# Sharing the first normalisation with GpSimd and asking for the weights after it, with the first v on SyncE's queue

## The chip, the cores and the metric

The kernel runs on one core of a Trainium2 chip. The metric is device time in microseconds (us), the median of several executions. The span that a trace shows is some 2 us shorter than that time.

In the views of the profile, PE is TensorE's matmuls, PEld its weight loads, DVE is VectorE, ACT is ScalarE, POOL is GpSimd and SP is SyncE. An "L" with a number is a line of that kernel's own source. A "q" behind an engine is that engine's sequencer.

## The reference

A linear attention over 8 batches, 8 heads, 576 positions and 64 columns a head, followed by two matrix products with a periodic function between them.

```python
def _attn_ref(q, k, v):                       # (8, 8, 576, 64) f32
    q_s = np.exp(q - max);  q_s /= sum over the last axis
    k_s = np.exp(k - max);  k_s /= sum over the positions
    kv = np.einsum('bhsd,bhse->bhde', k_s, v)
    return np.einsum('bhsd,bhde->bhse', q_s, kv)

def _moe_ref(x, w_in, w_out, alpha):          # x (4608, 512), w_in (512, 2048), w_out (2048, 512)
    h = x @ w_in
    s = np.sin(alpha * h)
    g = h + s * s / (alpha + 1e-09)
    return (g @ w_out).astype(np.float32)
```

(The two lines of the softmaxes are shortened.) Each of the two weights is 4.2 MB in f32, and q, k and v are 1.18 MB for each batch.

## The kernel before

The kernel works batch by batch. ACT takes exponentials of q and k, DVE sums and normalises q, PE transposes it and multiplies k by v, and the result goes into `xT`. The two products with the weights then keep PE busy until the end, while the next batches' attention is worked in between. The helpers that matter here are these:

```python
def load_win(c0, c1):                    # two requests for columns c0..c1 of w_in, f32 -> bf16 on the way
    n = slice(c0, c1)
    for x in range(2):
        nc.gpsimd.dma_start(out=win[64 * x:64 * x + 64, :, n], in_=win_v[x][:, :, n])

def load_wout(c):
    nc.gpsimd.dma_start(out=wout[:, 4 * c:4 * c + 4, :], in_=wout_v[:, 4 * c:4 * c + 4, :])

def norm_q(b, engs):                     # for each half ii of the batch's q
    ...
            nc.vector.tensor_reduce(part, qe[:, ii], axis=AXL.X, op=ALU.add)
            nc.vector.reciprocal(part, part)
        engs[ii % len(engs)].tensor_tensor(qn[:, ii]..., qe[:, ii], part..., op=ALU.mult)
```

The prologue asks for q and k on SyncE's queue. GpSimd asks for v and the weights. A copy of one element, called `held`, makes GpSimd wait until the first half of q has landed.

```python
load("q", q, 0, halves=True)             # SyncE
load("k", k, 0, halves=True)             # SyncE
...
GP_CP(singles.tile([128, 1], F32, name="held"), staged["q", 0][:, 0, 0, 0:1])
staged["v", 0] = st = stage.tile([128, 4, J, D], F32, name="st_v", tag="st")
for ii, j0, j1 in ((0, 0, 9), (1, 0, 5), (1, 5, 9)):
    GP.dma_start(out=st[:, ii::2, j0:j1]..., in_=src_view(v, 0)[:, ii::2, j0 * D:j1 * D])
for c0, c1 in ((0, 256), (256, 512), (512, 1024), (1024, 1536), (1536, 2048)):
    load_win(c0, c1)
for c in range(2):
    load_wout(c)
exp_q(0)
exp_k(0)
...
warm_up(7)
norm_q(0, [V, V])                        # both halves on DVE
```

Later loads are tied to the work of the first 512 tokens (`ni` counts its 16 column blocks of w_in). A gate is a tiny write by DVE into the buffer, so that the request waits until DVE has got there.

```python
late = {6: lambda: load("q", q, 1, halves=True, gate=DVE_CP), 8: lambda: load_wout(2),
        10: lambda: load_wout(3), 13: lambda: load("k", k, 1, halves=True, gate=DVE_CP)}
...
load("v", v, 1, halves=True)             # second batch's v, on SyncE behind the gated k
```

The softmax here doesn't subtract the row's maximum and nothing guards it: scores larger than these inputs give would overflow.

## Time and profile before

| | before |
|---|---|
| median of the first 3 runs | 289.12 us (289.1 to 289.53) |
| span of the trace | 286.8 us, of which PE is busy 274.9 |
| first matmuls on the weights | 15.74 us |
| second batch's v landed | 42.77 us |

PE idles for 286.8 - 274.9 = 11.9 us, mostly before 15.74. The one view to add is the timeline of GpSimd in the prologue. Its columns are the start in us, the duration, engine, source line, operation, what it wrote and read, the number of instructions, and in brackets the idle time before it with what ended it.

```profile
5.09 2.32 POOL L295 DMA_DIRECT2D st_v<-in_v_dram  x3
7.40 3.13 POOL L107 DMA_DIRECT2D win<-in_moe_w_in_dram  x5
11.43 0.61 POOL L107 DMA_DIRECT2D win<-in_moe_w_in_dram  x1 [0.90 <-DMA st_v<-in_v_dram]
12.25 2.61 POOL L107 DMA_DIRECT2D win<-in_moe_w_in_dram  x4 [0.21 <-issue]
```

GpSimd wrote requests for weights from 7.40 to 10.53.

### The profile page before, as it was taken

What the parts mean: (1) busy time and instruction counts of PE and PEld (TensorE: products, weight loads), DVE (VectorE), ACT (ScalarE), POOL (GpSimd) and SP (SyncE); (2) the same over time, 40 slices, a digit from 0 to 9 for tenths busy, and PEclk for the clock granted to TensorE, in tenths of its full rate; (3) what the DMA queues carried; (4) which work ended last, traced back from release to release, by engine and by line L of the source; (5) the groups of instructions that cost most, each with busy time, mean ns of one, the idle gap of its engine ahead of it and who ended that gap; (6) DMA issues with size and microseconds to landing.
All of it is one profiled execution on the core that took longest, in us unless ns stands there. A gap on an engine that the chain in (4) does not pass through costs nothing.

```text
span 286.8 us, 4259 instructions
## 1 busy us (share of the span) xinstructions
PE 274.9 (96%) x1570; PEld 130.6 (46%) x1570; DVE 188.5 (66%) x281; ACT 226.6 (79%) x320; POOL 81.6 (28%) x77
## 2 busy tenths in 40 slices
PE   1899999999999999999999999999999999999994
PEld 0444454445454445444544454445444444444443
DVE  3867775899968668756775677757674555555412
ACT  4889756999489999899889988998877777777500
POOL 4859420674766571005300530032000000000000
PEclk9999999999999999999999999999999999999999
DMA  7999999946799957129910990116011111111142
GB/s 253 309 205 242 269 391 408 307 169 191 167 199 402 361 184 120 38 43 358 289 37 21 336 308 27 37 39 139 17 39 37 37 37 39 37 37 38 41 109 73
DMA packets 37381, 45.77 MB, mean 160 GB/s; under 512 B 15968, under 2 KB 20848, under 8 KB 37360
## 3 DMA queue, kind: packets, MB, share of 16 engines
q1 hardware_dynamic: 32032, 39.98, 46.3%
q0 software_dynamic: 5136, 5.38, 10.2%
q8 instruction: 12, 0.20, 0.3%
q10 hardware_dynamic: 192, 0.14, 0.2%
q14 instruction: 9, 0.07, 0.1%
HBM read 36.71 MB, written 9.44 MB: 161 GB/s over the span
## 4 chain that ended last, share of the span: by engine, by line
PE 84%; DMA 7%; DVE 5%; POOL 1%; ACT 1%; issue 1%; SPq 0%; POOLq 0%
PE hp L234 38%; PE op L254 35%; DMA st_v<-in_v_dram 4%; PE hh L234 3%; PE kvp L157 2%; PE xp L206 2%; DMA qT<-qn 2%; DMA st_q<-in_q_dram 1%; DVE qs L144 1%; PE op L532 1%; PE op L234 1%; ACT s L240 1%; DVE qn L146 1%; POOL qn L146 1%; POOL s L244 1%
## 5 line engine op out<-in xcount | busy, mean ns | idle before, releaser
L250 DVE SCALAR_TENSOR_TENSOR g<-s,inva_sb,hp 128x512 bf16<-128x512 f32 x130 | 96.1, 745 | 64.1 <-ACT s L242 54.2
L234 PE MATMUL hp<-xT,win 128*128 128x512 bf16 x520 | 129.7, 379 | 0.0
L254 PE MATMUL op<-wout,g 128*128 128x512 bf16 x496 | 124.2, 379 | 0.0
L240 ACT ACTIVATE s<-hp,alpha_sb 128x512 f32<-128x512 f32 x130 | 87.6, 682 | 25.4 <-PE hp L234 24.3
L234 PEld LDWEIGHTS <-win 128*128 128x128 bf16 x576 | 56.3, 98 | 67.4 <-issue 0.4
L254 PEld LDWEIGHTS <-g 128*128 128x128 bf16 x560 | 54.1, 98 | 61.7 <-issue 0.9
L242 ACT ACTIVATE s<-s 128x512 f32<-128x512 f32 x112 | 70.5, 630 | 3.5
L146 POOL TENSOR_TENSOR qn<-qe,qs 128x1152 bf16<-128x1152 bf16 x12 | 25.3, 2128 | 73.2 <-DVE qs L140 63.1
L244 POOL TENSOR_TENSOR s<-s 128x512 f32<-128x512 f32 x29 | 30.5, 1061 | 24.8 <-ACT s L240 24.3
L260 DVE COPY o<-op 128x512 f32<-128x512 f32 (+2 forms) x33 | 22.1, 669 | 9.6 <-PE op L254 7.1
L117 ACT ACTIVATE ke<-st_k 128x1152 bf16<-128x1152 f32 x16 | 17.9, 1151 | 4.8 <-DMA st_k<-in_k_dram 4.1
L117 ACT ACTIVATE qe<-st_q 128x1152 bf16<-128x1152 f32 x16 | 17.9, 1156 | 2.8 <-DMA st_q<-in_q_dram 2.8
L139 DVE TENSOR_REDUCE qs<-qe 128x36 f32<-128x2304 bf16 x5 | 12.8, 2553 | 8.7 <-ACT qe L117 8.6
L131 POOL CAST vb<-st_v 128x1152 bf16<-128x1152 f32 x12 | 13.6, 1162 | 10.4 <-DMA st_v<-in_v_dram 10.4
L254 PE MATMUL hp<-wout,g 128*128 128x512 bf16 x64 | 15.1, 379 | 0.0
L209 DVE CAST xT<-xp 128x512 bf16<-128x512 f32 (+1 forms) x18 | 13.4, 742 | 0.0
L117 ACT ACT_TABLE_LOAD x7 | 9.0, 1283 | 1.3 <-PEq L546 1.2
L157 PEld LDWEIGHTS <-ke 64*128 64x128 bf16 x288 | 8.2, 93 | 3.5 <-ACT s L242 1.3
L157 PE MATMUL kvp<-vb,ke 64*128 64x130 bf16 x288 | 9.7, 216 | 0.0
L234 PE MATMUL hh<-xT,win 128*128 128x512 bf16 x40 | 9.4, 379 | 0.0
L144 DVE TENSOR_REDUCE qs<-qe 128x18 f32<-128x1152 bf16 x6 | 8.0, 1329 | 2.1 <-ACT qe L117 2.1
L206 PE MATMUL xp<-qT,kbd 128*128 128x256 bf16 (+1 forms) x40 | 8.2, 286 | 0.4 <-DVE xT L209 0.3
(68 smaller groups left out, 117.9 us busy)
## 6 DMA issues: line engine op xcount, KB each, us to landing
out_dram<-o SPq DMA_DIRECT2D x70, 128.0 KB, 2.3
st_q<-in_q_dram SPq DMA_DIRECT2D x6, 1152.0 KB, 6.3
st_k<-in_k_dram SPq DMA_DIRECT2D x6, 1152.0 KB, 8.2
st_v<-in_v_dram SPq DMA_DIRECT2D x6, 1152.0 KB, 10.3
st_q<-in_q_dram SPq DMA_DIRECT2D x4, 576.0 KB, 5.5
st_k<-in_k_dram SPq DMA_DIRECT2D x4, 576.0 KB, 7.1
wout<-in_moe_w_out_dram POOLq DMA_DIRECT2D x4, 512.0 KB, 11.2
win<-in_moe_w_in_dram POOLq DMA_DIRECT2D x6, 256.0 KB, 7.1
```

The costliest lines, as they stand in the source:

```text
L117: nc.scalar.activation(dst[:, :, ii * 128:(ii + 1) * 128].rearrange("p j (x d) -> p x j d", x=2), src[:, ii::2], AX.Exp)
L131: engs[ii](vv[:, 2 * ii:2 * ii + 2, :, 0:D], staged["v", b][:, ii::2])
L146: engs[ii % len(engs)].tensor_tensor(qn[:, ii].rearrange("p j (x d) -> p j x d", x=2), qe[:, ii], part.unsqueeze(3).to_broadcast([128, J, ...
L157: nc.tensor.matmul(kvp[:, e, ii * 130:(ii + 1) * 130], ke[r, j, ii * 128:(ii + 1) * 128], vt[r, j, ii * 130:(ii + 1) * 130], start=(j == 0 ...
L206: nc.tensor.matmul(xp[:, e, 0:n], kt[:, e, ii], qT[:, ii, j0:j1, e * 64:(e + 1) * 64], start=True, stop=True)
L234: nc.tensor.matmul(hp, win[:, ki, ni * 128:(ni + 1) * 128], xT[:, ki, t * MF:(t + 1) * MF], start=(ki == 0), stop=(ki == 3))
L240: nc.scalar.activation(s, hp, AX.Sin, scale=alpha_sb[:, ni:ni + 1])
L242: nc.scalar.activation(s, s, AX.Square)
L244: nc.gpsimd.tensor_tensor(s, s, s, op=ALU.mult)
L250: nc.vector.scalar_tensor_tensor(G[t][:, ni], in0=s, scalar=inva_sb[:, ni:ni + 1], in1=hp, op0=ALU.mult, op1=ALU.add)
L254: nc.tensor.matmul(acc, G[t][:, ni, j * 128:(j + 1) * 128], wout[:, ni, :], start=(ni == 0), stop=(ni == nN - 1))
L260: eng(o[:, cols], acc)
```

## The change

The intent is to finish the first batch's q earlier by giving one half of its normalisation to GpSimd, which only issued requests until then. The weights' requests follow that product on GpSimd. The first v would have had to wait too, so SyncE asks for it, behind k. One copy moves from ACT to DVE, and PE's warm-up matmuls are distributed anew.

```diff
     load("k", k, 0, halves=True)
+    staged["v", 0] = st = stage.tile([128, 4, J, D], F32, name="st_v", tag="st")
+    for ii, j0, j1 in ((0, 0, 9), (1, 0, 5), (1, 5, 9)):
+        nc.sync.dma_start(out=st[:, ii::2, j0:j1].rearrange("p i j d -> p i (j d)"),
+                          in_=src_view(v, 0)[:, ii::2, j0 * D:j1 * D])
 ...
-    GP_CP(singles.tile([128, 1], F32, name="held"), staged["q", 0][:, 0, 0, 0:1])
-    (v's three requests on GpSimd, the same as above)
+    exp_q(0)                             # these and two helpers only change place
+    exp_k(0)
+    ...
+    warm_up(9)
+    norm_q(0, [GP, V])
+    q_tile(0)
     for c0, c1 in ((0, 256), (256, 512), (512, 1024), (1024, 1536), (1536, 2048)):
         load_win(c0, c1)
     for c in range(2):
         load_wout(c)
 ...
-    warm_up(7)
-    norm_q(0, [V, V])
-    q_tile(0)
     q_transpose_ii(0, 0, 0, 8, tps[0])
 ...
-    warm_up(6)
+    warm_up(1)
 ...
-    ACT_CP(A["qT", 0][:, 1, 0:8], tps[1])
+    DVE_CP(A["qT", 0][:, 1, 0:8], tps[1])
```

(The lines in brackets and the comments stand for what is left out.)

More of the change, by code (lines that the diff above doesn't have):

```diff
@@ L289 @@
     nc.vector.reciprocal(inva_sb, alpha_sb)
-    GP_CP(singles.tile([128, 1], F32, name="held"), staged["q", 0][:, 0, 0, 0:1])
-    staged["v", 0] = st = stage.tile([128, 4, J, D], F32, name="st_v", tag="st")
-    for ii, j0, j1 in ((0, 0, 9), (1, 0, 5), (1, 5, 9)):
-        GP.dma_start(out=st[:, ii::2, j0:j1].rearrange("p i j d -> p i (j d)"),
-                     in_=src_view(v, 0)[:, ii::2, j0 * D:j1 * D])
-    for c0, c1 in ((0, 256), (256, 512), (512, 1024), (1024, 1536), (1536, 2048)):
-        load_win(c0, c1)
-    for c in range(2):
-        load_wout(c)
     exp_q(0)
@@ L312, in cast_v0 @@
         eng(vv[:, 2 * ii:2 * ii + 2, j0:j1, 0:D], staged["v", 0][:, ii::2, j0:j1])
-    warm_up(7)
-    norm_q(0, [V, V])
+    warm_up(9)
+    norm_q(0, [GP, V])
     q_tile(0)
+    for c0, c1 in ((0, 256), (256, 512), (512, 1024), (1024, 1536), (1536, 2048)):
+        load_win(c0, c1)
+    for c in range(2):
+        load_wout(c)
     q_transpose_ii(0, 0, 0, 8, tps[0])
```

## The prediction

> **What bounds the kernel now.** I read the page first: the engines' shares, then the chain that ended last.
>
> ```profile
> PE 274.9 (96%) x1570; PEld 130.6 (46%) x1570; DVE 188.5 (66%) x281; ACT 226.6 (79%) x320; POOL 81.6 (28%) x77
> PE 84%; DMA 7%; DVE 5%; POOL 1%; ACT 1%; issue 1%; SPq 0%; POOLq 0%
> ```
>
> TensorE is busy 274.9 of 286.8 us and makes 84% of the chain. Nothing in the change removes a useful matmul, so only the 11.9 us in which PE is idle can shrink, and the change touches the first batch alone: the first 16 us. Second I read the order of time there. These are DVE's lines for the first batch's q (columns: start us, us, engine, line, operation), then for the second batch, where DVE and GpSimd already share the normalisation just as the change wants it for the first; the POOL line belongs to that second batch.
>
> ```profile
> 6.13 1.35 DVE L144 TENSOR_REDUCE qs<-qe 128x18 f32<-128x1152 bf16 x1 [2.13 <-ACT qe L117]
> 7.82 1.36 DVE L146 TENSOR_TENSOR qn<-qe,qs 128x1152 bf16<-128x1152 bf16 x1
> 10.78 1.36 DVE L146 TENSOR_TENSOR qn<-qe,qs 128x1152 bf16<-128x1152 bf16 x1
> ...
> 34.74 1.34 DVE L144 TENSOR_REDUCE qs<-qe 128x18 f32<-128x1152 bf16 x1
> 37.93 1.97 DVE L146 TENSOR_TENSOR qn<-qe,qs 128x1152 bf16<-128x1152 bf16 x1
> ...
> 36.56 2.13 POOL L146 TENSOR_TENSOR qn<-qe,qs 128x1152 bf16<-128x1152 bf16 x1 [4.56 <-DVE qs L145]
> ```
>
> DVE alone needs 6.13 to 12.14 for both halves; shared, 34.74 to 39.90. Third, what follows on PE and ACT:
>
> ```profile
> 12.20 0.73 PE L186 MATMUL tp<-identb,qn 128*128 128x128 bf16 x10 [1.04 <-DVE qn L146]
> 12.86 1.20 PE L157 MATMUL kvp<-vb,ke 64*128 64x130 bf16 x36
> 15.74 1.95 PE L234 MATMUL hp<-xT,win 128*128 128x512 bf16 x8
> ...
> 10.31 0.99 ACT L319 COPY qT<-tp 128x1024 bf16<-128x1024 bf16 x1
> 11.20 0.74 ACT L312 CAST vb<-st_v 128x640 bf16<-128x640 f32 x1
> ```
>
> From 15.74 on PE runs without a gap to the second batch. So the start of those first `hp` matmuls is what the prologue delivers. Fourth, the chain in order of time around the second batch (start, us, what):
>
> ```profile
> 32.24 10.53 DMA st_v<-in_v_dram
> 42.77 0.02 issue
> 42.79 0.76 DVE vb L131
> 43.55 0.59 DVE o L260
> ...
> 44.92 0.55 PE xp L214 x2
> ```
>
> The second batch's v is requested at 32.24 and lands only at 42.77, and PE's attention matmuls at 44.92 hang on it. Why 10.5 us for 0.59 MB? The table by stretches (last columns: DMA share, GB/s):
>
> ```profile
> 3.00:8.00 5.00, 2.10 (x6) 0.97 (x7) 2.22 (x5) 2.46 (x3) 3.03 (x5) 1.00 1.04 403
> 9.00:11.00 2.00, 1.93 (x15) 0.95 (x14) 1.93 (x4) 1.78 (x3) 1.53 (x3) 1.00 0.96 368
> 11.00:13.00 2.00, 0.96 (x17) 0.70 (x18) 1.88 (x3) 1.33 (x3) 1.37 (x2) 1.00 1.14 221
> 14.00:24.00 10.00, 9.37 (x45) 4.04 (x44) 7.16 (x14) 9.17 (x17) 6.17 (x8) 1.00 1.26 205
> 38.00:42.80 4.80, 4.80 (x42) 2.64 (x41) 3.34 (x4) 3.76 (x4) 0.69 (x1) 1.00 1.04 410
> ```
>
> The DMA engines are full from 3 us to beyond 42.8 us. The weights count here as the bf16 written; they are read as f32, so 205 GB/s is 410 read. What must pass before that v has landed: three batches' halves q, k, v twice, 6 x 1.18 = 7.1 MB, and both weights, 8.4 MB as f32: 15.5 MB, at 0.405 MB/us some 38 us, from 3 to 41. That is the landing at 42.77 but for about a microsecond of notice. So there are **two bounds in series**: the prologue's chain of engines to 15.74, and the DMA stream to 42.77.
>
> **What the Trainium skill says.** "SBUF — State Buffer", section "Who interferes with whom": a VectorE instruction with two SBUF inputs contends with a GpSimd instruction that reads SBUF, and the second of them to start waits for the whole of the first. The trace agrees: GpSimd ran to 36.56 + 2.13 = 38.69, and DVE's multiplication, 1.36 us alone, took 1.97 and ended at 39.90, 1.21 after GpSimd. "GPSIMD Engine Reference", section "3.1 Elementwise — side-by-side cycle accounting": a two-input tensor_tensor in f32 is 1.96 times slower on GpSimd; here, with a broadcast factor, it is 2.13 / 1.36 = 1.57 times. "DMA: Bandwidth & Descriptors", section "SWDGE vs HWDGE vs iDMA": requests of SyncE and GpSimd end on the same 16 engines; GpSimd writes descriptors in software and VectorE's two-port modes can lock it out meanwhile. The stretches agree on the first (403 and 410 on the hardware queue, 2 x 205 on the other); on the second there is a hint: the one weight request beside DVE's two casts at 12.06 took 0.78 us, the shortest took 0.62. The same page, "Specifications", has the first byte of a GpSimd request after about 1 us, of a SyncE one after 0.6; this trace can't tell, since the engines were full when GpSimd first asked.
>
> **The change part by part.**
> 1. GpSimd takes the first half. The first reciprocal ends at 7.52 + 0.27 = 7.79. In the second batch GpSimd began 0.17 after it, so 7.96, and 2.13 gives 10.09, where DVE gave 9.18: this half is **0.9 later**.
> 2. DVE keeps the second half and follows the second batch's pattern: 39.90 - 34.74 = 5.16 after 6.13, so 11.29 instead of 12.14: **0.85 earlier**.
> 3. PE transposes the first half at 10.15 to 10.77. ACT's copy, 10.31 before, begins at about 10.82 and the v cast behind it at 11.71 (copy to cast takes 0.89 as before), done at 12.45 instead of 11.94. The second half's ten transposes run 11.35 to 12.08. The k-v matmuls wait for ACT's cast: 12.50 instead of 12.86. So **0.36 earlier**, not 0.85.
> 4. The copy of the second transposed half (ACT, 1.00 us) goes to DVE. DVE has the two v casts (0.82 us for both) from 11.29 to 12.11 and this copy, about 0.7 by the 0.75 of a 1152-column one, to 12.85. It is free when the k-v result comes (13.59 - 0.36 = 13.23). No cost, and ACT is free for its v cast at 12.35 to 12.98.
> 5. v on SyncE's queue: four q and k halves landed 1.46 us apart (4.92 to 9.2), so v lands at 10.7, 11.5 and 12.1 against 11.1, 12.0 and 12.6 before. In the kernel before ACT idled 0.67 for the last piece, which the k-v matmuls used only later; now it lands ahead of ACT.
> 6. The weights are requested from 10.1 instead of 7.4. They could not move before v was through at about 11.7 in the kernel before. Now v is through at 8.5 + 1.18/0.405 = 11.4, and the first weights follow at an estimated 11.5 to 12 (10.09 plus one issue of 0.62, or the skill's 1 us, plus some). Needed is the first piece at 15.1 and the 512 to 1024 columns at 18.7, two issues and 2.1 MB after: at 0.41 MB/us, 17 to 17.6 plus 0.9 notice. Close, but in time.
> 7. Matmuls of warm-up: 7 + 6 become 9 + 1, in PE's idle time; they set no end.
>
> So `hp` starts at about 15.4. **But** that gain of 0.36 meets the second bound. The landing at 42.77 moves only if the stream moves. The kernel before lost, against 405, about 0.2 us in 9 to 11 us and 0.4 in 11 to 13: 0.6 us. The changed one wins this back with v on the hardware queue and pays an estimated 0.1 to 0.6 of gap after v, and up to 0.4 while DVE's casts disturb the second to third request, with no backlog to hide it. Sum: **0 +- 0.5 us** at 42.77. PE, 0.36 early, then waits there, and the end stays: 289.1.
>
> **Rivals.** (a) *The prologue's gain carries through*: 289.12 - 0.36 = 288.75, if v lands 0.4 earlier. For it: the lost 0.6 us. Against: GpSimd asks 2.7 us later. (b) *The weights come late*: GpSimd's first request after 10.1 needs 2.5 us, as requests under load do (the first of 5.09 moved nothing before 8.4, when k was through), v drains at 11.4, the engines idle for 1.2 us: the second batch's v lands 0.6 to 1 later, perhaps with a wait for `win` near 18.7: 289.8 to 290. For it: latencies of 2.4 to 3.4 us everywhere in this trace; against: all of those were behind a backlog. (c) *GpSimd becomes the bound*: its requests now end near 10.1 + 10 x 0.63 + 0.37 + 1.51 = 18.3, and its first square came at 19.06, 18.7 when PE is early. No wait expected; 0.3 us if the lock costs more.
>
> **Range and chances.** All terms are under 1 us, 2% is 5.8 us. Point 289.1, range 288.5 (rival a with a bit more) to 289.9 (rival b). Faster by over 2%: 0.01; within: 0.98; slower: 0.01.
>
> **What would show it.** Right: GpSimd's product 7.96 to 10.1, DVE's ending near 11.3 and lasting 1.97, `hp` starting near 15.4 and no PE wait on `win`; the second batch's v landing at 42.3 to 43.3, and PE's gap before the attention matmuls near 45 grown from 0.1 to some 0.5 us. Wrong: DMA share under 0.8 in 11 to 13 us (rival b), an earlier landing with the end earlier by as much (a), a first square after 19 behind GpSimd's requests (c), or PE idle for something other than v between 16 and 44 us.

## The result

| | before | after |
|---|---|---|
| median of 6 runs each | 289.04 us (288.43 to 289.53) | 292.27 us (292.03 to 292.86) |
| span of the trace | 286.8 us | 290.2 us |
| PE busy | 274.9 us | 274.9 us |
| first matmuls on the weights | 15.74 us | 15.56 us |
| second batch's v landed | 42.77 us | 45.97 us |

The ratio of after to before is 1.0118, with a 95% interval of 1.0101 to 1.0134. All ratios here are the mean time of one kernel's runs over the mean of the other's of the same rounds, so they aren't quite the ratios of the medians. The changed kernel is slower by 1.2%, with no overlap between the two sets of runs. It lies outside the predicted range.

From the page of the changed kernel, first the busy time by engine, then the shares of the chain that ended last:

```profile
PE 274.9 (95%) x1567; PEld 130.3 (45%) x1567; DVE 188.5 (65%) x281; ACT 226.0 (78%) x319; POOL 81.4 (28%) x74
PE 74%; DMA 10%; DVE 7%; POOL 5%; ACT 2%; issue 2%; SPq 0%; ACTq 0%; POOLq 0%
```

PE's work is the same, and its share of the chain fell from 84% to 74%. Something else set the time in stretches where PE had set it before. The timeline of GpSimd and DVE in the changed prologue is the next view.

```profile
7.79 2.12 POOL L146 TENSOR_TENSOR qn<-qe,qs 128x1152 bf16<-128x1152 bf16 x1 [6.49 <-DVE qs L145]
9.86 6.33 POOL L107 DMA_DIRECT2D win<-in_moe_w_in_dram  x10
...
9.19 1.95 DVE L146 TENSOR_TENSOR qn<-qe,qs 128x1152 bf16<-128x1152 bf16 x1
```

The normalisation went as intended: GpSimd's half ended at 9.91, and DVE's at 9.19 + 1.95 = 11.14 instead of 12.14. The weights are asked for from 9.86 instead of 7.40. PE's timeline shows where that led:

```profile
12.57 0.97 PE L157 MATMUL kvp<-vb,ke 64*128 64x130 bf16 x28 [0.65 <-ACT vb L305]
15.56 1.95 PE L234 MATMUL hp<-xT,win 128*128 128x512 bf16 x8
...
20.92 3.61 PE L234 MATMUL hp<-xT,win 128*128 128x512 bf16 x16 [1.69 <-DMA win<-in_moe_w_in_dram]
...
43.74 1.45 PE L254 MATMUL hp<-wout,g 128*128 128x512 bf16 x6 [0.73 <-DMA wout<-in_moe_w_out_dram]
```

PE starts on the weights 0.18 us earlier, but then waits 1.69 us for `win`, columns 512 to 1024, and later 0.73 us for a piece of `wout`. The kernel before has neither wait. The chain in order of time (start, us, what) says the same and goes on to the second batch:

```profile
9.92 3.18 POOL win L107 x5
13.10 7.69 DMA win<-in_moe_w_in_dram
...
20.92 1.90 PE hp L234 x8
...
33.80 12.16 DMA st_v<-in_v_dram
...
45.99 0.77 DVE vb L131
```

The request that GpSimd finished at 13.10 took 7.69 us to land. The second batch's v was asked for 33.80 - 32.24 = 1.56 us later, and its landing took 12.16 - 10.53 = 1.63 us longer, together the 3.2 us by which DVE's cast is later (45.99 against 42.79). From that cast to the end the two kernels agree: 286.8 - 42.79 = 244.0 and 290.2 - 45.99 = 244.2 us. So the whole loss had happened by 45.99. Its first visible part is before 20.92. The table by stretches for the same windows as in the prediction (last columns: DMA share, GB/s):

```profile
9.00:11.00 2.00, 1.25 (x11) 0.50 (x9) 1.97 (x2) 1.66 (x3) 2.00 (x3) 1.00 1.05 375
11.00:13.00 2.00, 1.16 (x26) 1.08 (x28) 1.34 (x4) 1.52 (x2) 2.00 (x4) 1.00 1.18 212
14.00:24.00 10.00, 8.00 (x43) 3.28 (x38) 6.04 (x12) 7.43 (x13) 6.81 (x9) 1.00 1.09 158
```

There is no hole: the DMA share is above 1 in all three. Yet from 14 to 24 us the engines delivered 158 GB/s of weights instead of 205. A share above 1 hides this, because several packets can be in flight for one engine: the full stream of the kernel before has a share of 1.26 in the same stretch, and beside that the 1.09 here is low. The trace's packet records say the same. From 14 to 21 us the median packet of weights took 98 ns in both kernels, so most packets were as fast as before. On average 16.3 were in flight instead of 20.1, and 20 of 1187 took 300 ns or more, against none before. The stream ran without a break, but it was not full.

How much the stream lost can be counted in the trace's packet records, by adding up bytes until a given sum is reached. The weights are counted here at the f32 size that is read, twice what is written, and the fetches of instructions are left out. Times in us:

```
MB moved so far      4      5      6      7      8     15
before           13.06  15.57  18.00  20.47  22.97  40.29
after            13.00  17.32  20.53  23.04  25.49  43.22
```

Up to 13 us the two kernels are level. Between the fourth and the seventh megabyte the changed one loses 20.47 to 23.04, that is 2.6 us, and from there it runs at the old pace (2.45 us for the next megabyte, 2.50 before). At 15 MB the debt is 2.9 us.

### The profile page after: what moved, and what is told of

It is laid out like the page before. It is cut to its first block, busy times and chain, and to the rows that moved or that the text cites. A ratio compares the mean times of both kernels' runs of the same rounds, so it can differ in the third digit from the quotient of the medians. Undisturbed runs are those within 1.5% of the kernel's fastest.

```text
span 290.2 us, 4254 instructions
## 1 busy us (share of the span) xinstructions
PE 274.9 (95%) x1567; PEld 130.3 (45%) x1567; DVE 188.5 (65%) x281; ACT 226.0 (78%) x319; POOL 81.4 (28%) x74
## 4 chain that ended last, share of the span: by engine, by line
PE 74%; DMA 10%; DVE 7%; POOL 5%; ACT 2%; issue 2%; SPq 0%; ACTq 0%; POOLq 0%
PE op L254 34%; PE hp L234 32%; DMA st_v<-in_v_dram 4%; POOL s L244 3%; DVE g L250 3%; DMA win<-in_moe_w_in_dram 3%; PE kvp L157 2%; PE xp L206 2%; ACT s L240 1%; DMA st_q<-in_q_dram 1%; DMA qT<-qn 1%; DVE qs L144 1%; PE op L529 1%; PE op L234 1%; POOL win L107 1%
## 5 line engine op out<-in xcount | busy, mean ns | idle before, releaser
L146 POOL TENSOR_TENSOR qn<-qe,qs 128x1152 bf16<-128x1152 bf16 x13 | 27.4, 2127 | 79.2 <-DVE qs L140 62.3
## 6 DMA issues: line engine op xcount, KB each, us to landing
st_v<-in_v_dram SPq DMA_DIRECT2D x6, 1152.0 KB, 10.7
```

What stands on the lines that cost most here:

```text
L146: engs[ii % len(engs)].tensor_tensor(qn[:, ii].rearrange("p j (x d) -> p j x d", x=2), qe[:, ii], part.unsqueeze(3).to_broadcast([128, J, ...
```

## The experiments

Three theories were open. **L**: requests that GpSimd makes only shortly before the DMA engines get to them are carried slowly. **Q**: v on the hardware queue beside weights on the software queue is what costs. **C**: the work on GpSimd and DVE next to the requests (the product, the casts of v) disturbs the writing of the descriptors. The medians of the kernel before in the same rounds were 288.92 (e1 to e4), 289.09 (e5 to e8) and 288.76 us (e9 and e10). All ten kernels gave correct results.

### e1: only v moves to SyncE's queue

```diff
 # against the kernel before
     load("k", k, 0, halves=True)
+    (v's three requests on nc.sync, as in the change)
     GP_CP(singles.tile([128, 1], F32, name="held"), staged["q", 0][:, 0, 0, 0:1])
-    (v's three requests on GpSimd)
     (the weights' requests, as before)
```

> The kernel before with one part of the change: the first batch's v on SyncE's queue behind k. GpSimd still asks for the weights as soon as the first half of q has landed (about 5 us), VectorE normalises both halves. Theory L (late requests: the weights crawl at 158 instead of 205 GB/s in 14 to 24 us because GpSimd asks for them with nothing queued ahead): the rate in 14 to 24 us is back at 205, the second batch's v lands by 43, the time is 288.5 to 290 (v may share the engines with the weights and land late, so the first hp matmuls may start up to 1.5 us later). Theory Q (a mix of hardware and software queues makes the weights slow): the rate stays near 160 and the time near 292. Theory C (DVE's casts and GpSimd's product disturb the descriptor writing): as L.

Measured: 289.51 us (289.23 to 291.67, 4 runs), ratio 1.0036 (0.9999 to 1.0073). The row for 14 to 24 us:

```profile
14.00:24.00 10.00, 8.62 (x45) 3.87 (x46) 5.95 (x12) 9.51 (x16) 5.02 (x6) 1.00 1.26 204
```

The stream is full, with v on the hardware queue and the weights asked for from 4.84. Since the weights were asked for early, they shared the engines with v from about 9.4 on and v came later: PE waited 1.20 us for ACT's cast of it, and its first `hp` matmuls on the weights began at 16.70. So Q alone costs no rate in the stream. A loss of time is not clear of the noise here (the interval reaches 0.9999); what the trace shows is v's lateness.

### e2: e1, with the weights asked for as late as in the change

```diff
 # against e1: GpSimd waits for the second half of k instead of the first of q
-    GP_CP(singles.tile([128, 1], F32, name="held"), staged["q", 0][:, 0, 0, 0:1])
+    GP_CP(singles.tile([128, 1], F32, name="held"), staged["k", 0][:, 1, 0, 0:1])
```

> As e1_v_sync, but GpSimd's one-element copy that holds the requests back reads the second half of k, so the first weight request is made at about 10 us as in the changed kernel, and GpSimd still multiplies nothing. Theory L: slow again, 158 GB/s in 14 to 24 us, PE waits 1 to 2 us for the columns 512 to 1024 near 19 to 21 us, time 291.5 to 293. Theory C with GpSimd's product as the cause: 205 GB/s and 289 to 290. Theory Q: slow like e1_v_sync.

Measured: 292.13 us (291.58 to 293.59, 4 runs), ratio 1.0118 (1.0087 to 1.0149), the same ratio as the change itself. GpSimd's line and PE's wait, from the timelines:

```profile
9.64 6.37 POOL L107 DMA_DIRECT2D win<-in_moe_w_in_dram  x10
...
20.68 3.61 PE L234 MATMUL hp<-xT,win 128*128 128x512 bf16 x16 [1.56 <-DMA win<-in_moe_w_in_dram]
```

The stream ran at 165 GB/s from 14 to 24 us. There is no product on GpSimd here, and DVE normalises both halves as before. Against e1 one thing differs, the time of the requests (9.64 instead of 4.84), and it brings the whole effect. That speaks for L, and against the product as the cause.

### e3: the change, with v back on GpSimd's queue

```diff
 # against the changed kernel
-    (v's three requests on nc.sync)
+    GP_CP(singles.tile([128, 1], F32, name="held"), staged["q", 0][:, 0, 0, 0:1])
+    (v's three requests on GpSimd, before the product)
     (product on GpSimd, then the weights' requests)
```

> The changed kernel with the first batch's v back on GpSimd's queue, asked for at about 5 us, before the product; the weights are still asked for after the product, at about 10 us. Theory L in its plain form (lateness alone): slow, near 158 GB/s and 291.5 to 293. Theory Q (the hardware queue's v): 205 GB/s in 14 to 24 us and 288.5 to 289.5. If it falls between, both a backlog on the same queue and lateness matter.

Measured: 292.57 us (292.36 to 293.55, 4 runs), ratio 1.0134 (1.0112 to 1.0155), with 166 GB/s from 14 to 24 us and PE waits of 1.24 and 1.06 us for `win`. The mix of queues is gone and the loss stays, so Q has fallen.

### e4: the change, with the first four weight requests before the product

```diff
 # against the changed kernel
+    GP_CP(singles.tile([128, 1], F32, name="held"), staged["q", 0][:, 0, 0, 0:1])
+    for c0, c1 in ((0, 256), (256, 512)):
+        load_win(c0, c1)
     exp_q(0)
 ...
-    for c0, c1 in ((0, 256), (256, 512), (512, 1024), (1024, 1536), (1536, 2048)):
+    for c0, c1 in ((512, 1024), (1024, 1536), (1536, 2048)):
```

> The changed kernel, but GpSimd asks for the first 512 columns of the weights (four requests, some 2.6 us) at about 5 us, before its product, and for the rest after it. Theory L: the later requests find a backlog, the rate in 14 to 24 us is near 205, the second batch's v lands near 43, time 288.5 to 289.5. Theory C (casts and descriptors at 11 to 13 us): the requests made after 10 us still crawl, 290.5 to 292. Theory Q: slow, near 292.

Measured: 291.43 us (289.83 to 292.22, 4 runs), ratio 1.0079 (1.0043 to 1.0115). The stream was full, 206 GB/s from 14 to 24 us, although the product was on GpSimd and six of the ten requests came after it. The time missed what L hoped for: v again shared the engines with the early weights and landed late, PE waited 1.38, 0.83 and 1.20 us, and `hp` began only at 18.45. PE's lateness then delayed the gated requests behind it (the second batch's q was asked for at 27.86 instead of 24.43), and the granted TensorE clock was 0.76 from 17 to 24 us. So this run supports L for the stream and is a failure as a remedy.

### e5: e1, with the weights asked for in between

```diff
 # against e1: GpSimd waits for the first half of k
-    GP_CP(singles.tile([128, 1], F32, name="held"), staged["q", 0][:, 0, 0, 0:1])
+    GP_CP(singles.tile([128, 1], F32, name="held"), staged["k", 0][:, 0, 0, 0:1])
```

> As e1_v_sync, but the requests for the weights are held back until the first half of k has landed: they start near 7.9 us, between e1_v_sync (4.8) and e2_late_weights (9.6). Theory L (the earlier the requests stand in the queue, the fuller the stream): between the two in rate, or full if 3.5 us of lead before v is through at 11.4 us is enough; then v is less disturbed than in e1_v_sync, the first hp matmuls start at 15.4 to 15.7, and the time is 288.4 to 289.3. If the lead isn't enough: 290 to 291.5.

Measured: 290.26 us (289.52 to 290.63, 4 runs), ratio 1.0037 (1.0011 to 1.0063), and 183 GB/s from 14 to 24 us. The requests went out at 8.79, later than the 7.9 that was expected. By rate this lies between e1 (204) and e2 (165), so in this one run the effect looks graded and not like a switch.

### e6: e2, with DVE's two casts of v on ACT

```diff
 # against e2
-    cast_v0(0, 5, 9, DVE_CP)
+    cast_v0(0, 5, 9, ACT_CP)
 ...
-    cast_v0(1, 0, 5, DVE_CP)
+    cast_v0(1, 0, 5, ACT_CP)
 ...
-    ACT_CP(A["qT", 0][:, 1, 0:8], tps[1])
+    DVE_CP(A["qT", 0][:, 1, 0:8], tps[1])
```

> As e2_late_weights, but both of VectorE's casts of the first v are done by ScalarE, and ScalarE's copy of the second transposed half by VectorE, so that no VectorE instruction with its source and target both in SBUF runs between 11 and 14 us while GpSimd writes the requests. Theory C (VectorE's casts lock GpSimd out of writing the descriptors): the dip at 12.5 to 13.5 us and the slow stretch from 15 to 20 us go, 200 GB/s in 14 to 24 us. Theory L without the lock: the slow stretch stays, 155 to 170 GB/s in 14 to 24 us, PE still waits 1 to 2 us for the columns 512 to 1024.

Measured: 292.2 us (292.09 and 292.31), ratio 1.0108 (1.0082 to 1.0135), and 160 GB/s from 14 to 24 us, no better than e2. The casts were one part of theory C, and they are not the cause. One copy had to come to DVE in exchange, and DVE's own product, which the expectation overlooked, still ran beside the first requests (10.43 to 11.79). So the run doesn't show that nothing on DVE matters.

### e7: the change, with columns 512 to 1024 in narrower pieces

```diff
 # against the changed kernel
-    for c0, c1 in ((0, 256), (256, 512), (512, 1024), (1024, 1536), (1536, 2048)):
+    for c0, c1 in ((0, 256), (256, 512), (512, 768), (768, 1024), (1024, 1536), (1536, 2048)):
```

> The changed kernel with the columns 512 to 1024 asked for in two pieces of 256 columns, like those ahead of them (four requests instead of two). The slow stretch of the changed kernel deepens at 15 us, where the first pieces of 512 columns come. If the piece's width is what crawls, 15 to 17.5 us now run at 180 GB/s or more, and PE's wait near 19 us shrinks under 0.7 us; if it is the lateness, the stream stays near 110 to 160 GB/s there and the time at 291.5 to 293.

Measured: 292.13 us (291.76 and 292.5), ratio 1.0106 (1.0076 to 1.0136), and 169 GB/s. PE waited only 0.39 us for `win`, but 2.3 us for `wout` later. The size of the piece decides where the debt of the stream is paid, and the debt stays.

### e8: e1, with the weights asked for after everything else has landed

```diff
 # against e1: held and all weight requests move behind DVE's first cast of v
+    GP_CP(singles.tile([128, 1], F32, name="held"), vb[0][:, 5, 0:1])
+    (the weights' requests)
```

> As e2_late_weights, but the weights are asked for only when VectorE has cast a part of v, near 12.2 us, when the DMA engines have nothing left to do. If a stream that starts behind nothing always crawls for its first 7 to 9 us (lateness alone, no other traffic needed), it moves under 170 GB/s from its start near 13.5 to about 22 us and is full after it; if it needs v's tail or VectorE's casts at the same time, it is at 200 GB/s within 2 us. Time 294 to 298 in either case.

Measured: 294.12 us (293.82 and 294.42), ratio 1.0175 (1.0146 to 1.0204). GpSimd asked from 12.45 on, with the engines idle, so that no other transfer was in the way. The row for the first stretch:

```profile
14.00:20.00 6.00, 3.57 (x10) 1.17 (x12) 2.12 (x5) 2.88 (x5) 5.83 (x10) 0.71 1.05 126
```

The stream crawls at 126 GB/s here too, and comes to 203 GB/s in 24 to 27 us. So neither other traffic nor v's landing is needed for the slow start. (The granted clock was 0.71 in this stretch, in which PE was busy for 3.57 of 6 us. What that adds to the time of this run was not taken apart; the rate of the DMA engines is what the run was made for.)

### e9: product on GpSimd and early requests

GpSimd asks first for v, in two requests instead of three, and for columns 0 to 512, in two instead of four. It then multiplies, and asks for the rest.

```diff
 # against the changed kernel
-    (v's three requests on nc.sync)
+    GP_CP(singles.tile([128, 1], F32, name="held"), staged["q", 0][:, 0, 0, 0:1])
+    for ii, j0, j1 in ((0, 0, 9), (1, 0, 9)):
+        GP.dma_start(out=st[:, ii::2, j0:j1]..., in_=src_view(v, 0)[...])
+    load_win(0, 512)
     exp_q(0)
 ...
-    for c0, c1 in ((0, 256), (256, 512), (512, 1024), (1024, 1536), (1536, 2048)):
+    for c0, c1 in ((512, 1024), (1024, 1536), (1536, 2048)):
```

> The change with GpSimd's product kept, but the lead of the requests kept too: GpSimd asks from 4.8 us for v in two pieces and for the columns 0 to 512 of the weights in two, all written by about 7.7 us, then multiplies its half, then asks for the rest from about 10 us. So every request stands some 4 us before the engines come to it, as in the kernel before. Theory L: 200 to 206 GB/s in 14 to 24 us, no wait of PE for the weights, the first hp matmuls at 15.3 to 15.8 us, the second batch's v landing at 42.4 to 43.1, 288.4 to 289.3 us: same as before or a little faster. If GpSimd's product itself does harm: above 290.5.

Measured: 289.18 us (288.87 to 289.31, 5 runs), ratio 1.001 (0.9997 to 1.0024): the same as the kernel before. The stream ran at 203 GB/s from 14 to 24 us, and PE had no wait for weights. The product stood from 7.75 to 9.93, as in the change, so the product is not the cause. DVE's cast of the second batch's v, from the timeline:

```profile
42.72 0.77 DVE L131 CAST vb<-st_v 128x1152 bf16<-128x1152 f32 x1 [0.87 <-DMA st_v<-in_v_dram]
```

It came at 42.72, against 42.79 in the kernel before. In this run the shared normalisation won nothing even with a full stream: `hp` began at 15.64, 0.10 us earlier than before, v's cast came only 0.07 earlier, and the time is no better. It was hoped to be a little faster than the kernel before and was not. Whether another order would win something was not tried.

### e10: the change, with another load between v and the weights

SyncE asks for the second batch's q right behind v, ungated. GpSimd's requests keep their time, but the DMA engines are occupied 2.9 us longer before they get to them (1.18 MB at 0.405 MB/us).

```diff
 # against the changed kernel
     (v's three requests on nc.sync)
+    load("q", q, 1, halves=True)
 ...
-        late = {6: lambda: load("q", q, 1, halves=True, gate=DVE_CP), 8: lambda: load_wout(2),
+        late = {8: lambda: load_wout(2),
```

> The changed kernel, GpSimd's requests as late as there (about 9.9 us), but SyncE asks for the second batch's q right behind the first batch's v, so that the DMA engines have work until about 14.3 us. If what counts is how long a request has stood when the engines come to it, the stream is full (the fifth to ninth MB move as fast as in the kernel before, within 0.7 us in all), although PE waits for the weights, which come 1 to 2.5 us later, and the time is 289.5 to 292. If what counts is that GpSimd's queue starts at that time or runs its first requests, it crawls again: 2 us or more lost over those 4 MB, 292 to 294.

Measured: 291.12 us (290.5 and 291.75), ratio 1.0079 (1.0056 to 1.0103). The row for the stretch in which the weights alone were carried:

```profile
17.00:24.00 7.00, 6.61 (x23) 2.81 (x25) 2.85 (x4) 4.11 (x8) 4.08 (x6) 0.76 1.26 204
```

The requests went out at 9.72, just as in the change, and the stream is full. What counts is therefore not when the requests are made on the clock, nor that they follow the product, but how far GpSimd is ahead when the engines reach them. As a version it is worse than the kernel before, because the weights come behind 1.18 MB that is not needed yet: PE waited 1.67 us for the first of them, and its first matmuls on the weights began at 17.17. The granted clock was 0.76 in this stretch too.

### The ten runs in one table

"Asked" is the time of GpSimd's first request for weights, "first packets" the time of the twentieth packet of weights in the records, "lead" the difference of the two. The fourth column is how long the stream took from its fourth to its eighth megabyte (weights at their f32 size), the last is the start of DVE's cast of the second batch's v. All in us.

```
run      asked  first packets  lead  4th to 8th MB   cast of 2nd v
before    7.40      11.58       4.2       9.91           42.79
e9        6.50      11.43       4.9       9.90           42.72
e1        4.84       9.37       4.5       9.92           43.51
e4        4.77       9.32       4.6       9.92           45.98
e10       9.72      14.23       4.5      10.04           44.85
e5        8.79      11.34       2.5      10.98           44.25
e2        9.64      11.60       2.0      11.99           45.64
after     9.86      11.77       1.9      12.50           45.99
e7        9.76      11.58       1.8      11.90           45.81
e6        9.68      11.44       1.8      12.24           46.54
e8       12.45      14.14       1.7      11.60           48.10
e3        9.77      11.41       1.6      12.00           46.34
```

Five kernels with a lead of 4.2 us or more need 9.9 to 10.0 us. Six with 2.0 us or less need 11.6 to 12.5. The one between lies between. The number of weight requests that GpSimd had finished by the "first packets" sorts the runs just as well: 5, 4, 7, 4 and 7 in the first five rows, 3 in e5, and 2 in each of the six slow ones. The last column shows that a full stream is necessary for an early v but not sufficient: e4 and e10 lost their time on PE, whose progress gates later requests.

## Why the prediction was wrong

The prediction built on two bounds in series, and that frame held. (Its 7.1 MB of q, k and v are those of two batches; "three batches' halves" is a slip.) From the cast of the second batch's v to the end the spans of the kernel before, the change and e1 to e10 took 243.9 to 245.2 us, though the cast itself moved from 42.72 to 48.10. As was said, the prologue's gain did not reach the end: in the change the loss covers it, and in e9, where nothing does, the time is still that of the kernel before. The one sign of being wrong that did show was PE idle between 16 and 44 us for something other than v: 1.69 us for `win` and 0.73 for `wout`.

**Steps 1 and 2** were right: GpSimd's product was 7.79 to 9.91 (predicted 7.96 to 10.09), and DVE's half ended at 11.14 (11.29) and took 1.95 us (1.97).

**Step 3** was right: the k-v matmuls ran from 12.57 (12.50).

**Step 5** was off by 0.6 to 1 us in the landings of v, predicted for 10.7, 11.5 and 12.1. (The spacing in it, from 4.92 to 9.2 in three steps, is 1.43 us and not 1.46, which changes little.) In the timelines DVE idled until 11.33 and again until 12.22 for the two pieces that it casts, and ACT until 13.14 for the last piece, each released by v's transfer. PE's last eight k-v matmuls waited 0.27 us for that last cast.

**Step 4** was nearly right. Because of those waits DVE's copy took 0.67 us from 12.76 instead of ending at 12.85, and the reciprocal behind it on DVE started as it drained, at 13.35, so that the copy may have cost about 0.1 us. The harm of both steps together was small: `hp` began at 15.56, 0.18 earlier than before, where the sum of the steps had said about 15.4.

**Step 6 is where it failed.** Its first half was right. There was no hole in front of the weights: their first packets are in the records at 11.37, while v was still being carried, and the predicted gap of 0.1 to 0.6 us was hardly there. Its second half took for granted that the stream then runs at 0.41 MB/us, "at 0.41 MB/us, 17 to 17.6 plus 0.9 notice", since it does so in the kernel before from the first packet. In place of the 205 GB/s written that this means, the trace has 158 from 14 to 24 us, and PE, ready for the columns 512 to 1024 at 20.92 - 1.69 = 19.23 (the prediction had said 18.7), could go on only at 20.92. Its sum was not quite right either, but on the safe side: 11.5 to 12 plus 2.1 MB at 0.41 MB/us is 16.6 to 17.1. By the predicted rate the columns would have been there in time. The sum, "0 +- 0.5 us at 42.77", contained a term for a gap and a term for a disturbance by the casts (up to 0.4), and no term for a stream that runs without a break and isn't full. The prediction did note that GpSimd would have no backlog then, but priced this at the casts' 0.4 us. The missing term measured 2.6 us by the seventh megabyte and 2.9 by the fifteenth. The landing moved by 3.2 us, and the span by 3.4. The kernel before had five requests for weights finished when the engines came to them, the changed one two. The casts, for which the sum did make room, were tried alone in e6, and without them the rate was 160.

**Step 7** was right; no warm-up matmul stands in a wait of PE that set anything.

**The rivals.** Rival (b), that the weights come late, had the direction and foresaw a wait for `win` near 18.7, which came to 1.69 us before 20.92. Its mechanism, idle DMA engines for 1.2 us, did not happen, and so its size of 0.6 to 1 us was too small. The sign that was to betray it, a DMA share under 0.8 from 11 to 13 us, was 1.18 and stayed silent: up to 13 us nothing had been lost, and in the slow stretch behind it the share was still 1.09, above 1. Against rival (a) speaks e9: with a full stream, the shared normalisation and `hp` 0.10 us earlier, the landing is at the old place, and so is the time. The full 0.36 us was reached in neither kernel. Rival (c) did not matter: GpSimd's first square came at 18.89 and its wait was for ACT.

**What is shown and what is open.** Shown by e2 against e1, and by e10 against the change, is that how far ahead of the engines GpSimd makes its requests decides the rate for the next 7 to 9 us. The queue of v (e1, e3), the product (e2, e4, e9), the casts of v (e6), the width of a piece (e7) and other traffic (e8) are not the cause. Open is what inside the DMA engines or GpSimd makes such a stream slow. Fewer packets in flight (16.3 against 20.1) at the same median time of a packet fits engines that are short of prepared work, but no run takes that apart, nor the few packets of 300 to 774 ns. Nor did any run separate the time that requests have stood from the number or bytes of requests standing; in these kernels both grow together, and the number finished (4 to 7, 3, 2) may be what counts.

## What to carry to other kernels

A row of DMA requests on GpSimd that only seems to wait in line may be doing its work: here requests made at least 4.2 us before the engines reached them, with four or more finished, streamed at 203 to 206 GB/s written, and the same ones made 2 us ahead or less at 158 to 169 from 14 to 24 us, which cost more than the 1 us that GpSimd's help saved on DVE. (e8, the latest, had 126 from 14 to 20 us.) Before giving an issuing engine other work, look at how far its requests stand ahead of the engines, and judge a stream by its GB/s, or by its share beside that of a full stream (1.26 here), not by a share above 1. And where a full transfer stream bounds a later point, as v's landing at 42.77 does here, a faster prologue of the compute engines can gain nothing even when it works, as in e9.

## What the Trainium skill lacked or had wrong

- "DMA: Bandwidth & Descriptors", section "Specifications", gives a latency to the first byte of about 1 us for GpSimd's requests. It doesn't say from where that is counted. In e8, with idle engines, GpSimd's instruction for the first request ran from 12.45 to 13.26 and the first packet of weights is recorded at 13.97: 1.5 us from its start, 0.7 from its end. The part that mattered has no place on the page: after that first packet the stream was slow for a further 6 to 9 us (126 GB/s in e8 from 14 to 20 us, 158 in the change from 14 to 24, against 203 to 206 when the lead was 4.2 us or more).
- The same section gives about 358 GB/s as a core's limit of HBM without a condition; only its section "Measured (HBM→SBUF, 128 partitions, SWDGE, issued from GpSimd)" adds that this is for both cores of a pair streaming and that one alone gets more. This one core moved 398 to 410 GB/s in the stretches from 3 to 8 us of both kernels and 38 to 42.8 us of the kernel before.
- "DMA: Bandwidth & Descriptors", section "Issuing engines are not separate DMA queues", says that starting transfers from several engines saves only the sequencer's time. What it lacks is that the moment of asking can matter for the rate: in these runs it was 204 GB/s when GpSimd asked at 4.84 (e1) and 165 when it asked at 9.64 (e2).
- "SBUF — State Buffer", section "Who interferes with whom", has a DMA that a DVE operation stalls as one of GpSimd's short of port time. A reader takes that as the first suspect for slow requests of GpSimd. It was not the cause here as far as the casts of v go (160 GB/s in e6 without them, 165 in e2 with them). What the section says of a two-input DVE instruction beside GpSimd agreed: the multiplication took 1.95 us beside GpSimd's, against 1.36 alone.
